# An attention and mixture-of-experts kernel on one core: all sixteen head pairs kept in the rotated column order of memory

## The chip, the cores and the metric
The kernel runs on one core of one Trainium2 chip. The metric is device time in microseconds (us) from launch to end. TensorE is called PE below (PEld is its weight load), VectorE is DVE, ScalarE is ACT, GpSimd is POOL; SyncE (SP) only issues DMAs. SBUF is the on-chip memory of 128 partitions, PSUM the eight accumulator banks that PE writes.

## The reference
Inputs are float32: q, k, v of shape (4, 8, 576, 64), that is 4 batches of 8 heads. Cut to what matters:

```python
q_rot, k_rot = rotate(q), rotate(k)            # rotary embedding: two products and a sum per element
scores = scale * q_rot @ k_rot.T               # per head, 576 x 576
attn = exp(scores - rowmax); attn /= attn.sum(-1) + 1e-9
x = (attn @ v) as (2304 tokens, 512)
logits = x @ phi                               # 32 slots
slots = softmax over tokens(logits).T @ x      # then 8 experts, w1 relu w2, on 4 slots each
x = softmax over slots(logits) @ slot_out
out = relu(x @ w_in) ** 2 @ w_out              # 512 -> 2048 -> 512, 2304 tokens
```

## The kernel before, in words
The 32 heads are worked as sixteen pairs (`p` = 0 to 15, four pairs a batch): the even head of a pair lies on partitions 0 to 63, the odd head on 64 to 127, with the 576 positions along the columns. The work of a pair:

- `load` brings k, q and their swapped halves into one of two buffers `raws[p % 2]`, and `load_v` brings v into `vraws[p % 2]`. All are issued from SP.
- `rope_pair` (six 128x576 operations on POOL) rotates, `parts_pair` splits the result into a rounded part `hi` (ACT) and a rest `lo` (POOL).
- `max_unit` (L535) makes scores from `hi` alone, nine units a pair, and DVE takes their row maxima (L546); `max_rows` (L558 to L584) turns these into a row that a DMA brings back to SBUF (`mrow`).
- `st_unit` (L607, L614) makes the full scores less the maximum, and ACT takes the exponent (L627). Nine units a pair.
- `pv_unit` (L655, and L650 for the last 64 keys of both heads) multiplies by v into two accumulator banks: `obank0` (printed obank_94) for query columns 0 to 287, `obank1` (obank_95) for 288 to 575. These halves are called h = 0 and h = 1. The L650 unit of the next pair opens the accumulation in obank1.
- `norm` for each half: PE sums the exponents (L676), DVE transposes the sums (L682), inverts them (L688 to L691), transposes back (L702), and `scaled` (L698) multiplies the accumulator by the inverse and writes `xT`.
- `logits`: PE multiplies `xT` by phi (L726, L731) and transposes it (L749); after every fourth pair `slots_in` (L780 to L854) folds the batch into the slots.

The maximum, score, sum, logit and transpose units share a ring of three two-bank PSUM buffers (printed bank_91 to bank_93). A unit can start only when the reader of an earlier one has released a buffer.

The host stores the odd head's columns rotated by 64: key positions 512 to 575 come first, so that the two heads' 64-wide tails fall on different partitions. Pairs 0 to 3 (`p < TURNED`, `TURNED = 4`) stay in that order on chip. Their `load` is one DMA over all 128 partitions; their `load_v` is six DMAs that move runs of 256 bytes; `scaled` turns the odd head back as it writes `xT`, in three instructions for h = 0 (64x288, 64x64, 64x224) and two for h = 1 (64x288 each). Their rotary table, in the same order, lies in an extra buffer that a weight slot lends (`claim("w7")`, printed w__134). Pairs 4 to 15 are turned as they are loaded: three DMAs of 64 partitions each (`SEGS`), one contiguous DMA for v, one 128x288 instruction for `scaled`, and a second rotary table brought by `natural_table` (L1109) after the first maxima.

What sets the order: every operation is handed to `Plan.op` with an engine, a cost and a due time. `Plan.retime` shifts the due times by numbers in `UNITS`, `TABLE` and `SHIFT`; `Plan.emit` then issues the operations greedily: of those that could start next, the one due first, where an operation that keeps PE in its present kind of work (`mode`) gains `STAY`. The kinds are r (maxima and scores), c (value products), q (sums, logits, slots) and f (transposes). What results is one fixed instruction list per engine. The same planner places `prepare`, eight conversions of double-precision weights beside the pairs from the fourth on, each with two DVE steps (L1053, L1065), and the weight loads (`free`, L1002).

After the pairs come the experts and the two large products of the last layer (L1659), which use neither the rotary tables nor the pairs' buffers.

Of the kernel before, what the change touches and what calls it, by code (L numbers as in the profile page):

```python
# [9 lines left out]
F32 = mybir.dt.float32  # L10
# [9 lines left out]
B, H, S, D = 4, 8, 576, 64  # L20
# [18 lines left out]
class Plan:  # L39
# [8 lines left out]
    GAP = 0.5  # L48
    LEAVE = 0.09
    ENTER = {"r": 0.11, "c": 0.05, "q": 0.03, "f": 0.05, "b": 0.07, None: 0.05}  # L50
    STAY = 20.522
    AHEAD = 0.208
    UNITS = {
        ("st_unit", "PE", "r"): ("st", 0.0, 0), ("st_unit", "ACT", None): ("st", -9.501, 0), ("pv_unit", "PE", "c"): ("pv", 0.0, 0),
        ("max_unit", "PE", "r"): ("mx", 0.0, 13), ("max_unit", "DVE", None): ("mx", -58.652, 13),
    }
    TABLE = {
# [5 lines left out]
    }  # L63
    SHIFT = {
        ("norm", "PE", "q", False): 5.334,
        ("norm", "DVE", None, False): -51.924,
        ("logits", "PE", "q", False): 1.283,
        ("logits", "PE", "f", False): 3.961,
        ("logits", "DVE", None, False): -5.107,
        ("logits", "ACT", None, False): 1.109,  # L70
        ("max_rows", "PE", "f", False): -1.5,
        ("max_rows", "DVE", None, False): -14.126,
        ("slots_in", "PE", "f", False): 3.47,
        ("slots_in", "PE", "q", False): 2.384,
        ("slots_in", "DVE", None, False): -0.857,
        ("slots_in", "ACT", None, False): -1.093,
        ("rope_pair", "POOL", None, False): 1.035,
        ("parts_pair", "ACT", None, False): 0.251,
        ("parts_pair", "POOL", None, False): -1.618,
        ("load_v", "SP", None, False): 0.738,  # L80
        ("load", "SP", None, False): 0.879,
        ("st_unit", "POOL", None, False): -1.049,
        ("windows", "ACT", None, False): 0.494,
        ("norm", "PE", "q", True): 0.475,
        ("norm", "DVE", None, True): 1.892,
        ("logits", "PE", "q", True): 0.0,
        ("logits", "PE", "f", True): 0.0,
        ("logits", "DVE", None, True): 0.373,
        ("logits", "ACT", None, True): -1.901,
        ("slots_in", "PE", "f", True): -1.785,  # L90
        ("slots_in", "PE", "q", True): 0.0,
        ("slots_in", "DVE", None, True): 2.47,
        ("slots_in", "ACT", None, True): -0.248,
    }
    kind = None

# [167 lines left out]
def kernel(  # L264
# [104 lines left out]
    def dma(fn, due, kb, reads=(), writes=(), after=None, on="SP", behind=None):  # L369
        return op({on: 0.5}, lambda e: fn(), due, reads, writes, kb=kb, after=after, behind=behind)  # L370
# [26 lines left out]

    TURNED = 4  # L400
    early = []
    SEGS = ((slice(0, 64), slice(0, S), slice(0, S)), (slice(64, 128), slice(0, 512), slice(64, S)), (slice(64, 128), slice(512, S), slice(0, 64)))

    def load(p, g, ts_, on="SP", after=None, first="SP"):

        i = p % 2
        if p < TURNED:
            dma(
                lambda: QUEUE[on].dma_start(out=raws[i][:, ts_, :], in_=qk[p][:, ts_, :]),
                g, 1152 * len(range(4)[ts_]) / 4, (), [("raw", i, t, s) for t in range(4)[ts_] for s in range(3)], on=on, after=after,  # L410
            )
            return
        for s, (rows, to, of) in enumerate(SEGS):
            q = on if s else first
            dma(
                lambda rows=rows, to=to, of=of, q=q: QUEUE[q].dma_start(
                    out=raws[i][rows, ts_, to], in_=qk[p][rows, ts_, of]
                ),
                g + 0.01 * s, 1100 * len(range(4)[ts_]) / 4 * (to.stop - to.start) / S, (),
                [("raw", i, t, s) for t in range(4)[ts_]], on=q, after=after,  # L420
            )

    def tt(e, o, x, y, how):
        ENG[e].tensor_tensor(out=o, in0=x, in1=y, op=how)  # L424
# [3 lines left out]
    def rope_pair(p, g):  # L428

        i = p % 2  # L430
        on = {"POOL": 1.39} if p else {"DVE": 0.72}
        if p < TURNED:
            table, tk = (lambda t: early[0][0]()[:, t, :]), [[early[0][1]]] * 2
        else:
            table, tk = (lambda t: rope_sb[:, t, :]), [[("rope", t, s) for s in range(3)] for t in range(2)]
        first = {1: [("hi", 0, 1)], 2: [("mrow", 0, 0), ("mrow", 0, 1)]}.get(p, [])
        for t in range(2):
            a, b = raws[i][:, t, :], raws[i][:, t + 2, :]
            ka, kb = ([("raw", i, n, s) for s in range(3)] for n in (t, t + 2))
# [643 lines left out]
    def at(g, fn, *a):  # L1083
        todo.setdefault(g, []).append((fn, a))
# [4 lines left out]
        return group * first - shift + 0.05 * more  # L1089

    def first_loads():
        ((tab_of, tab_k),) = claim("w7", ([128, 2, S], F32))
        early.append((tab_of, tab_k))
        load(0, -99, slice(0, 4, 2))
        dma(lambda: nc.scalar.dma_start(out=tab_of(), in_=rope.rearrange("t r c -> r t c")), -98.9, 576, (), [tab_k], on="ACT")
        load(0, -98, slice(1, 4, 2))
        load(1, -97, slice(0, 4))
        dma(lambda: nc.sync.dma_start(out=ident, in_=ident_in), -96.5, 65, (), ["ident"])
# [4 lines left out]

        op({"DVE": 0.3}, apart, -20, ["ident"], ["apart"])

    def natural_table():
        for n, (rows, to, of) in enumerate(SEGS):
            dma(
                lambda rows=rows, to=to, of=of: nc.sync.dma_start(out=rope_sb[rows, :, to], in_=rope[:, rows, of].rearrange("t r c -> r t c")),  # L1109
                -2 + 0.01 * n, 550 * (to.stop - to.start) / S, (), [("rope", t, n) for t in range(2)], behind=rows_done[0],  # L1110
            )

    at(-100, first_loads)
    at(-4.1, natural_table)
    at(-4.2, lambda: op({"SP": 1.3}, lambda e: load_consts(), -7, (), ["phi"], kb=200, behind=rows_done[0]))
    for p in range(NP):
        g0 = NU * p
# [707 lines left out]
```

## Time and profile before

| what | value |
|---|---|
| three runs | 572.42, 572.80, 574.49 us; median 572.8 |
| the profiled execution | 571.77 us, span 570.0 us between first and last instruction |
| TensorE clock, mean | 0.991 of full speed |
| first full-score matmul (L607) | 20.17 us |
| last transposes of the pairs (L749) | 290.08 us |
| experts' first products (L1375) | 296.52 us |
| last layer's second product (L1659) | from 342.79 us to the end |

The pairs take some 270 us of the 570. The profile lists instructions per engine with start and duration; `[idle ...]` behind a row is the time for which the engine had stood still and what released it. A busy time of PE includes the tails of pipelined matmuls, so small pauses between units show in start times rather than as idle time.

### The profile page before, as it was taken

What the parts mean: (1) busy time and instruction counts of PE and PEld (TensorE: products, weight loads), DVE (VectorE), ACT (ScalarE), POOL (GpSimd) and SP (SyncE); (2) the same over time, 40 slices, a digit from 0 to 9 for tenths busy, and PEclk for the clock granted to TensorE, in tenths of its full rate; (3) what the DMA queues carried; (4) which work ended last, traced back from release to release, by engine and by line L of the source; (5) the groups of instructions that cost most, each with busy time, mean ns of one, the idle gap of its engine ahead of it and who ended that gap; (6) DMA issues with size and microseconds to landing.
All of it is one profiled execution on the core that took longest, in us unless ns stands there. A gap on an engine that the chain in (4) does not pass through costs nothing.

```text
span 570.0 us, 13340 instructions
## 1 busy us (share of the span) xinstructions
PE 551.7 (97%) x5486; PEld 421.8 (74%) x5486; DVE 384.7 (67%) x836; ACT 283.1 (50%) x528; POOL 220.2 (39%) x173
## 2 busy tenths in 40 slices
PE   3999999999999999999999999999999999999996
PEld 2656666576666667666643358999999999999996
DVE  6587788888888878776475129954784495454553
ACT  2334455654555664534423138964944564444440
POOL 4999999987888888621200000000000000000000
PEclk9699999999999999999999999999999999999999
DMA  6547796867785356245679997222200120000333
GB/s 235 152 125 189 169 238 181 228 174 212 194 228 118 102 135 180 96 174 176 218 258 386 387 396 272 75 75 75 75 1 1 75 75 1 0 2 1 112 112 112
DMA packets 41838, 85.69 MB, mean 150 GB/s; under 512 B 12176, under 2 KB 12848, under 8 KB 40624
## 3 DMA queue, kind: packets, MB, share of 16 engines
q1 hardware_dynamic: 41494, 84.24, 47.6%
q8 instruction: 43, 0.70, 0.5%
q10 hardware_dynamic: 282, 0.59, 0.3%
q14 instruction: 19, 0.16, 0.1%
HBM read 77.92 MB, written 6.82 MB: 149 GB/s over the span
## 4 chain that ended last, share of the span: by engine, by line
PE 89%; DVE 6%; DMA 1%; issue 1%; ACT 1%; SPq 0%; DVEq 0%; ACTq 0%
PE bank L1659 35%; PE obank L655 11%; PE bank L607 11%; PE bank L676 6%; PE bank L535 5%; PE bank L614 3%; DVE mcol L546 3%; PE obank L1589 3%; PE bank L1375 3%; PE bank L1437 2%; PE obank L650 2%; PE bank L749 2%; DMA ident<-in_ident_dram 1%; PE bank L726 1%; PE obank L1521 1%
## 5 line engine op out<-in xcount | busy, mean ns | idle before, releaser
L627 ACT ACTIVATE tO<-bank 128x576 f32<-128x576 f32 x144 | 86.3, 650 | 87.1 <-PE bank L614 82.9
L546 DVE TENSOR_REDUCE mcol<-bank 128x2 f32<-128x576 f32 x144 | 103.1, 747 | 20.5 <-ACT tO L627 9.5
L424 POOL TENSOR_TENSOR arena<-arena 128x576 f32<-128x576 f32 x78 | 110.9, 1443 | 7.9 <-DMA arena<-in_qk_dram 7.1
L1659 PE MATMUL bank<-w,tEb 128*128 128x256 f32 x864 | 106.4, 279 | 0.0
L1659 PEld LDWEIGHTS bank<-w,tEb 128*128 128x128 f32 x864 | 103.3, 188 | 2.4 <-issue 1.6
L655 PE MATMUL obank<-tO,pb 128*64 128x288 f32 x512 | 76.3, 419 | 0.0
L635 POOL TENSOR_TENSOR pb<-tO 128x576 f32<-128x576 f32 x32 | 45.9, 1434 | 36.4 <-ACT tO L627 34.7
L1659 PE MATMUL bank<-w,tEa 128*128 128x256 f32 x432 | 53.0, 279 | 0.0
L1659 PEld LDWEIGHTS bank<-w,tEa 128*128 128x128 f32 x432 | 51.6, 188 | 1.0 <-issue 0.8
L1659 PE MATMUL bank<-w,tO 128*128 128x256 f32 x432 | 51.5, 277 | 0.0
L1659 PEld LDWEIGHTS bank<-w,tO 128*128 128x128 f32 x432 | 51.0, 188 | 0.0
L655 PEld LDWEIGHTS obank<-tO,pb 128*64 128x64 f32 x512 | 31.2, 136 | 23.8 <-issue 9.2
L1600 ACT ACTIVATE pb<-obank 128x384 f32<-128x384 f32 x47 | 21.8, 496 | 44.0 <-PE obank L1589 44.0
L1600 ACT ACTIVATE w__1093<-obank 128x384 f32<-128x384 f32 x48 | 21.7, 494 | 36.4 <-PE obank L1589 36.3
L676 PE MATMUL bank<-tO,ones 128*32 128x288 f32 x256 | 36.7, 409 | 0.0
L535 PEld LDWEIGHTS bank<-tEb 64*128 64x128 f32 x180 | 16.3, 184 | 21.9 <-ACT tO L627 4.5
L535 PE MATMUL bank<-tEb 64*128 64x288 f32 x180 | 30.8, 356 | 1.1 <-ACT tO L627 0.5
L424 POOL TENSOR_TENSOR tLb<-arena,tEb 128x576 fp32r<-128x576 f32 x20 | 28.5, 1438 | 1.4 <-ACT tEb L458 1.4
L607 PE MATMUL bank<-tEb 64*128 64x288 f32 x180 | 28.2, 310 | 0.3 <-DVE mcol L546 0.2
L1589 PE MATMUL obank<-x,tO 128*128 128x384 f32 x95 | 27.0, 339 | 0.3 <-DVE tO L1533 0.3
L682 DVE STREAM_TRANSPOSE bank<-bank 128x288 f32<-128x288 f32 x32 | 15.9, 497 | 15.9 <-PE bank L676 15.8
L607 PE MATMUL bank<-tLb,tEb 64*128 64x288 f32 x180 | 26.6, 292 | 0.0
(301 smaller groups left out, 1064.2 us busy)
## 6 DMA issues: line engine op xcount, KB each, us to landing
arena<-in_qk_dram SPq DMA_DIRECT2D x14, 576.0 KB
arena<-in_qk_dram SPq DMA_DIRECT2D x12, 512.0 KB
arena<-in_w_dram SPq DMA_DIRECT2D x8, 512.0 KB
pb<-in_v_dram SPq DMA_DIRECT2D x12, 320.0 KB
arena<-in_qk_dram SPq DMA_DIRECT2D x3, 1152.0 KB
tLb<-in_w_in_dram SPq DMA_DIRECT2D x3, 1024.0 KB
pb<-in_w_in_dram SPq DMA_DIRECT2D x3, 1024.0 KB
w__450<-in_w_dram SPq DMA_DIRECT2D x4, 512.0 KB
```

The costliest lines, as they stand in the source:

```text
L424: ENG[e].tensor_tensor(out=o, in0=x, in1=y, op=how)
L535: nc.tensor.matmul(on_ring(tok)[:, j, 0:HQ], lhsT=x[rows], rhs=hi[rows, 0, HALF[c]], start=(u < BOTH or c == 0), stop=(u < BOTH or c == 1),)
L546: lambda e: nc.vector.tensor_reduce(out=mcol[:, h, :, u], in_=on_ring(tok)[:, :, 0:HQ], op=ALU.max, axis=AX.X),
L607: nc.tensor.matmul(st[:, j, 0:HQ], lhsT=w[rows], rhs=q[y][rows, HALF[c]], start=(i == 0 and (u < BOTH or c == 0)), stop=False,)
L614: nc.tensor.matmul(st[:, j, 0:HQ], lhsT=pick[rows, w : w + 128], rhs=mrow[rows, HALF[c]], start=False, stop=(u < BOTH or c == 1),)
L627: lambda e: nc.scalar.activation(out=pr, in_=on_ring(tok)[:, :, 0:HQ], func=AF.Exp, scale=0.125),
L635: lambda e: nc.gpsimd.tensor_tensor(out=acc, in0=one, in1=pr, op=ALU.add),
L655: nc.tensor.matmul(BANKS[6 + h][o, 0:HQ], lhsT=vr[:, u, j, :], rhs=pr[:, j, :], start=(h == 0 and u == 0), stop=(h == 1 and u == 3))
L676: nc.tensor.matmul(sm[QUAD[2 * j + w], 0:HQ], lhsT=one, rhs=xs_[2 * i + w][:, j, :], start=(i == 0), stop=(i == 1))
L1589: lambda e, i=i, t0=t0: nc.tensor.matmul(BANKS[i][:, 0:384], lhsT=wst_of()[:, 128 * fc : 128 * fc + 128], rhs=cst_of()[:, t0 : t0 + 384], ...
L1600: lambda e, i=i, h=h: nc.scalar.activation(out=rg_of()[:, 0, h], in_=BANKS[i][:, 0:384], func=AF.Relu),
L1659: nc.tensor.matmul(BANKS[c][:, cols], lhsT=gt[:, x, 128 * c : 128 * c + 128], rhs=wo[:, fc % 2, y, cols], start=(fc % FQ == 0 and i == 0 a ...
```

## The change
`TURNED` becomes `NP` (16). So every pair is loaded by one DMA over all partitions, every v by six DMAs, and every `scaled` is three instructions (h = 0) or two (h = 1). The branch with `SEGS` in `load` goes; its two other users (`natural_table`, and the choice of table in `rope_pair`) go too, and the one rotary table is loaded straight into its final place. The planner's numbers are replaced as a whole. The last layer is as before; the printed line numbers of the changed kernel are lower by 13 to 25.

```diff
-    STAY = 20.522
-    AHEAD = 0.208
+    STAY = 38.746
+    AHEAD = 0.207
...
-        "mx": (0.265, 1.712, 4.344, 4.474, 3.597, 2.052, 4.445, 5.88, 1.071),
+        "mx": (8.916, 13.853, 9.584, 11.633, 10.129, 5.789, 11.309, 14.53, 8.455),
...
-        ("load_v", "SP", None, False): 0.738,
+        ("load_v", "SP", None, False): -5.293,
...
-    TURNED = 4
-    early = []
+    TURNED = NP
...
             return
-        for s, (rows, to, of) in enumerate(SEGS):
-            q = on if s else first
-            dma(
-                lambda rows=rows, to=to, of=of, q=q: QUEUE[q].dma_start(
-                    out=raws[i][rows, ts_, to], in_=qk[p][rows, ts_, of]
-                ),
...
-        if p < TURNED:
-            table, tk = (lambda t: early[0][0]()[:, t, :]), [[early[0][1]]] * 2
-        else:
-            table, tk = (lambda t: rope_sb[:, t, :]), [[("rope", t, s) for s in range(3)] for t in range(2)]
+        table, tk = (lambda t: rope_sb[:, t, :]), [[("rope", t, s) for s in range(3)] for t in range(2)]
...
-        ((tab_of, tab_k),) = claim("w7", ([128, 2, S], F32))
-        early.append((tab_of, tab_k))
         load(0, -99, slice(0, 4, 2))
-        dma(lambda: nc.scalar.dma_start(out=tab_of(), in_=rope.rearrange("t r c -> r t c")), -98.9, 576, (), [tab_k], on="ACT")
+        dma(lambda: nc.scalar.dma_start(out=rope_sb, in_=rope.rearrange("t r c -> r t c")), -98.9, 576, (), [("rope", t, s) for t in range(2) for s in range(3)], on="ACT")
...
-    def natural_table():
-        for n, (rows, to, of) in enumerate(SEGS):
...
-    at(-4.1, natural_table)
```

PE, around the first maximum units of pair 2 (`tEb` holds its `hi`; rows of L535 write one maximum unit each, obank rows are value products). Before:

```order
L607 MATMUL bank_93<-tEb 128x288 x2
L607 MATMUL bank_93<-tLb,tEb 128x288 x2
L607 MATMUL bank_93<-tEb,tLb 128x288 x2
L614 MATMUL bank_93<-tEa,pick 128x288 x2
L535 MATMUL bank_92<-tEb 128x288 x2
L535 MATMUL bank_91<-tEb 128x288 x2
L535 MATMUL bank_93<-tEb 128x288 x2
L655 MATMUL obank_94<-tO_83,pb 64x288 x4
L535 MATMUL bank_92<-tEb 128x288 x2
```

The same place now (L520 is the maximum unit, L640 the value product, L661 the sums, L592 and L599 the scores):

```order
L661 MATMUL bank_93<-tO_84,half_ones 32x288
L640 MATMUL obank_95<-tO_83,pb 64x288 x2
L520 MATMUL bank_91<-tEb 128x288 x2
L520 MATMUL bank_92<-tEb 128x288 x2
L520 MATMUL bank_93<-tEb 128x288 x2
L520 MATMUL bank_91<-tEb 128x288 x2
L592 MATMUL bank_92<-tEb 128x288 x2
L592 MATMUL bank_92<-tLb,tEb 128x288 x2
L592 MATMUL bank_92<-tEb,tLb 128x288 x2
L599 MATMUL bank_92<-tEa,pick 128x288 x2
```

Two score units stood ahead of three maxima and a value product behind them; now four maxima stand in a row right behind a half's sums, and the scores follow.

DVE, the second half of pair 7 from the inversion of its sums to its logits (r_89 the inverse, mrow_124 the row of maxima, w__1093 or w__1058 the weight conversion). Before:

```order
L690 TENSOR_TENSOR r_89<-r_89,bank_92 32x9 x4
L691 RECIPROCAL r_89<-r_89 128x9
L546 TENSOR_REDUCE mcol_122<-bank_93 128x2
L702 STREAM_TRANSPOSE pb<-r_89 128x288
L558 TENSOR_REDUCE m_115<-mcol_122 128x10
L698 TENSOR_TENSOR pb<-obank_95,pb 128x288
L546 TENSOR_REDUCE mcol_119<-bank_92 128x2
L571 TENSOR_SCALAR mrow_124<-bank_93 10x128
L576 SCALAR_TENSOR_TENSOR mrow_124<-bank_93,keep_apart,mrow_124 10x64
L738 TENSOR_TENSOR lg_74<-lg_74,bank_92 128x192
```

And now:

```order
L675 TENSOR_TENSOR r_89<-r_89,bank_91 32x9 x4
L676 RECIPROCAL r_89<-r_89 128x9
L531 TENSOR_REDUCE mcol_122<-bank_92 128x2
L687 STREAM_TRANSPOSE pb<-r_89 128x288
L543 TENSOR_REDUCE m_115<-mcol_122 128x10
L683 TENSOR_TENSOR pb<-obank_95,pb 64x288 x2
L531 TENSOR_REDUCE mcol_119<-bank_91 128x2
L556 TENSOR_SCALAR mrow_124<-bank_92 10x128
L561 SCALAR_TENSOR_TENSOR mrow_124<-bank_92,keep_apart,mrow_124 10x64
L1050 SCALAR_TENSOR_TENSOR w__1058<-w__1058 128x512
L723 TENSOR_TENSOR lg_74<-lg_74,bank_91 128x192
```

The scaling became two instructions, and the second step of the weight conversion, which stood ahead of this half's first transpose, now stands between the row of maxima and the logits.

DVE at the end of the last pair (obank_95 is its second half, lg_76 the last batch's logits). Before:

```order
L698 TENSOR_TENSOR pb<-obank_94,pb 128x288
L702 STREAM_TRANSPOSE pb<-r_89 128x288
L698 TENSOR_TENSOR pb<-obank_95,pb 128x288
L738 TENSOR_TENSOR lg_76<-lg_76,bank_91 128x192
L780 TENSOR_REDUCE m_126<-lg_76 128x1
```

And now:

```order
L683 TENSOR_TENSOR pb<-obank_94,pb 64x288
L683 TENSOR_TENSOR pb<-obank_94,pb 64x64
L683 TENSOR_TENSOR pb<-obank_94,pb 64x224
L687 STREAM_TRANSPOSE pb<-r_89 128x288
L683 TENSOR_TENSOR pb<-obank_95,pb 64x288 x2
L723 TENSOR_TENSOR lg_76<-lg_76,bank_92 128x192
L765 TENSOR_REDUCE m_126<-lg_76 128x1
```

Nothing else changed place here: five scaling instructions stand where two stood.

## Rows read from the trace of the kernel before

**Rows 1.** The page's busy times: us, share of the span, instructions.

```profile
PE 551.7 (97%) x5486; PEld 421.8 (74%) x5486; DVE 384.7 (67%) x836; ACT 283.1 (50%) x528; POOL 220.2 (39%) x173
```

**Rows 2.** Chain of waits in order of time: start, us, what.

```profile
20.24 1.02 PE bank L607 x6
...
77.56 1.11 PE bank L676 x16
...
94.34 1.11 PE bank L676 x16
...
129.66 1.11 PE bank L676 x16
...
145.89 1.11 PE bank L676 x16
...
162.03 1.11 PE bank L676 x16
...
179.98 1.11 PE bank L676 x16
...
290.15 0.71 PE bank L749 x5
```

**Rows 3.** Busy times by stretch: stretch, us, per engine; clock, DMA share, GB/s.

```profile
51.20:68.60 17.40, 17.27 (x203) 10.64 (x196) 13.53 (x35) 7.63 (x16) 17.40 (x14) 1.00 0.64 150
...
145.89:162.03 16.14, 16.14 (x198) 10.73 (x202) 13.42 (x34) 10.30 (x19) 14.02 (x11) 1.00 0.75 208
```

**Rows 4.** Timeline, pair 2's maxima: start, us, engine, line, what, count.

```profile
40.25 0.94 PE L535 MATMUL bank<-tEb 64*128 64x288 f32 x6 [0.24 <-ACT tO L627]
...
41.15 6.08 DVE L546 TENSOR_REDUCE mcol<-bank 128x2 f32<-128x576 f32 x9
...
43.96 0.40 PE L535 MATMUL bank<-tEb 64*128 64x288 f32 x2 [0.27 <-DVE mcol L546]
...
45.29 0.82 PE L535 MATMUL bank<-tEb 64*128 64x288 f32 x4 [0.20 <-DVE mcol L546]
```

**Rows 5.** Groups by line and shape: the scaling; busy, mean ns.

```profile
L698 DVE TENSOR_TENSOR pb<-obank,pb 128x288 f32<-128x288 f32 x24 | 10.9, 454 | 6.0 <-PE obank L655 5.8
L698 DVE TENSOR_TENSOR pb<-obank,pb 64x288 f32<-64x288 f32 x12 | 5.4, 451 | 0.2
L698 DVE TENSOR_TENSOR pb<-obank,pb 64x224 f32<-64x224 f32 x4 | 1.5, 387 | 0.0
L698 DVE TENSOR_TENSOR pb<-obank,pb 64x64 f32<-64x64 f32 x4 | 0.9, 228 | 0.1
```

**Rows 6.** Timeline, pair 7's second half.

```profile
163.36 0.48 DVE L682 STREAM_TRANSPOSE bank<-bank 128x288 f32<-128x288 f32 x1
...
167.39 0.46 DVE L698 TENSOR_TENSOR pb<-obank,pb 128x288 f32<-128x288 f32 x1
...
168.42 0.71 PE L650 MATMUL obank<-tO,pb 64*64 64x288 f32 x8
...
169.18 0.75 PE L749 MATMUL bank<-ident,pb 128*128 128x128 f32 x5
```

**Rows 7.** Timeline, pair 2's second half.

```profile
82.79 0.92 DVE L698 TENSOR_TENSOR pb<-obank,pb 64x288 f32<-64x288 f32 x2
...
83.92 0.72 PE L650 MATMUL obank<-tO,pb 64*64 64x288 f32 x8
```

**Rows 8.** Timeline, the last pair's end.

```profile
289.11 0.46 DVE L698 TENSOR_TENSOR pb<-obank,pb 128x288 f32<-128x288 f32 x1 [1.10 <-PE obank L655]
...
289.62 0.30 PE L726 MATMUL bank<-pb,phi_sb 128*32 128x128 f32 x2 [0.22 <-DVE pb L698]
```

**Rows 9.** DMA issues of v on SP: count, ns min/median/max, first and last start.

```profile
L477 SPq DMA_DIRECT2D pb<-in_v_dram x24: 465/603/1737, 3.4 to 61.6; - x24
L482 SPq DMA_DIRECT2D pb<-in_v_dram x12: 327/328/342, 76.0 to 261.0; - x12
```

**Rows 10.** Waits of the SP queue: us in total, times, longest.

```profile
SPq L584 <- DVE mrow L576: 63.1, 16, 8.2
```

More of the change, by code (lines that the diff above doesn't have):

```diff
@@ L50 @@
     ENTER = {"r": 0.11, "c": 0.05, "q": 0.03, "f": 0.05, "b": 0.07, None: 0.05}
-    STAY = 20.522
-    AHEAD = 0.208
+    STAY = 38.746
+    AHEAD = 0.207
     UNITS = {
-        ("st_unit", "PE", "r"): ("st", 0.0, 0), ("st_unit", "ACT", None): ("st", -9.501, 0), ("pv_unit", "PE", "c"): ("pv", 0.0, 0),
-        ("max_unit", "PE", "r"): ("mx", 0.0, 13), ("max_unit", "DVE", None): ("mx", -58.652, 13),
+        ("st_unit", "PE", "r"): ("st", 0.0, 0), ("st_unit", "ACT", None): ("st", -53.91, 0), ("pv_unit", "PE", "c"): ("pv", 0.0, 0),
+        ("max_unit", "PE", "r"): ("mx", 0.0, 13), ("max_unit", "DVE", None): ("mx", -87.016, 13),
@@ L56 @@
     }
     TABLE = {
[5 rows of a table removed]
[5 rows of a table added]
     }
     SHIFT = {
[L65 to L79, printed above, removed]
-        ("load_v", "SP", None, False): 0.738,
[L81 to L85, printed above, removed]
+        ("norm", "PE", "q", False): 12.303,
@@ new lines @@
+        ("norm", "DVE", None, False): -42.242,
+        ("logits", "PE", "f", False): 9.173,
+        ("logits", "DVE", None, False): 1.345,
+        ("max_rows", "PE", "f", False): -1.538,
+        ("max_rows", "DVE", None, False): -14.332,
+        ("slots_in", "PE", "f", False): 10.484,
+        ("slots_in", "PE", "q", False): 0.192,
+        ("slots_in", "DVE", None, False): -0.45,
+        ("slots_in", "ACT", None, False): -0.389,
+        ("rope_pair", "POOL", None, False): 3.281,
+        ("parts_pair", "ACT", None, False): 1.349,
@@ L86 @@
+        ("parts_pair", "POOL", None, False): 5.432,
+        ("load_v", "SP", None, False): -5.293,
+        ("load", "SP", None, False): 0.952,
+        ("st_unit", "POOL", None, False): 2.631,
+        ("windows", "ACT", None, False): -2.946,
+        ("norm", "PE", "q", True): -2.865,
+        ("norm", "DVE", None, True): 1.214,
         ("logits", "PE", "q", True): 0.0,
         ("logits", "PE", "f", True): 0.0,
-        ("logits", "DVE", None, True): 0.373,
-        ("logits", "ACT", None, True): -1.901,
@@ L90 @@
[L90 to L93, printed above, removed]
+        ("logits", "DVE", None, True): 0.405,
+        ("logits", "ACT", None, True): 0.0,
+        ("slots_in", "PE", "f", True): 0.2,
+        ("slots_in", "PE", "q", True): -0.935,
+        ("slots_in", "DVE", None, True): 0.66,
+        ("slots_in", "ACT", None, True): 0.0,
     }
@@ L412, in load @@
             return
-        for s, (rows, to, of) in enumerate(SEGS):
-            q = on if s else first
-            dma(
-                lambda rows=rows, to=to, of=of, q=q: QUEUE[q].dma_start(
-                    out=raws[i][rows, ts_, to], in_=qk[p][rows, ts_, of]
-                ),
-                g + 0.01 * s, 1100 * len(range(4)[ts_]) / 4 * (to.stop - to.start) / S, (),
-                [("raw", i, t, s) for t in range(4)[ts_]], on=q, after=after,
-            )
     def tt(e, o, x, y, how):
@@ L1104, in first_loads @@
         op({"DVE": 0.3}, apart, -20, ["ident"], ["apart"])
-    def natural_table():
-        for n, (rows, to, of) in enumerate(SEGS):
[L1108 to L1111, printed above, removed]
     at(-100, first_loads)
-    at(-4.1, natural_table)
     at(-4.2, lambda: op({"SP": 1.3}, lambda e: load_consts(), -7, (), ["phi"], kb=200, behind=rows_done[0]))
```

8 rows, old and new, of the table TABLE are left out of this document.

## The prediction

> **What bounds the kernel now.** I read the page's busy times first: PE works for 97% of the span, no other engine for more than 74% of it [rows 1]. So the question is what PE's list costs and where PE pauses. The chain of waits in order of time answers both, since the same unit of a pair returns once a pair. Between the sums at 129.66, 145.89 and 162.03 lie 16.23 and 16.14 us [rows 2]. In the second of these stretches PE is busy for 16.14 of 16.14 us and DVE for 13.42 [rows 3]; I take 16.14 as the price of one pair with nothing lost. The step from 162.03 to 179.98 is 17.95, so folding a batch into the slots adds 1.81. From the first scores (20.24) to the last transposes (290.15) are 269.9 us; sixteen pairs and three such folds make 16 x 16.14 + 3 x 1.81 = 263.7. The rest, 6.2 us, is the ramp at both ends and the pauses, and it is all that the change could win among the pairs, unless it shortened PE's list.
>
> It doesn't. I counted PE's units in both instruction lists: the same number of each, and 207 changes of kind (r, c, q, f) where 208 stood. From the fourth pair on the two lists hold the same units per pair, with neighbours swapped here and there. So the forecast is a sum of pauses.
>
> Where the pauses are: 77.56 to 94.34 is 16.78, 0.64 too long; 94.34 to 129.66 is 35.32, which is two pairs, one fold and 1.23; 129.66 to 145.89 is 0.09 too long. That makes 1.96 us in pairs 3 to 6. Before that, at pair 2's maxima, PE stands idle for 0.24 + 0.27 + 0.20 = 0.71 us, waiting for buffers of the ring, while DVE works through nine maxima without a gap (6.08 us, 0.68 each) [rows 4].
>
> **The change part by part.** *Loads.* For twelve pairs three qk DMAs become one and one v DMA becomes six. An issue of v took 603 ns in the six-part form and 328 ns as one [rows 9], so SP gains at most 6 x 0.60 - 0.33 = 3.3 us a pair, less two qk issues. SP's list also carries the row of maxima that the next pair's scores need; there SP stood waiting for 63.1 us in 16 times, 3.9 each [rows 10], so the 3.3 fit in front of it. I take 0. If a v piece should stand blocked ahead of that row, the scores would wait; the bound from the other side is those 3.3 us twelve times, which I find far off, because the 3.9 would have to be gone.
>
> On the DMA engines the pairs with contiguous v moved 208 GB/s at a busy share of 0.75, those with v in pieces 150 GB/s at 0.64 [rows 3]: 277 against 234 GB/s per full share. Were all traffic of a pair as slow as the second, 208 x 16.14 = 3360 KB would take 14.3 us of 16.14, still less than the pair. The Trainium skill speaks against this part: DMA: Bandwidth & Descriptors (Specifications) wants runs of at least 512 bytes for line rate, and the new v runs are 256. By its rule alone DMA time grows; the row agrees in direction, and as the share stays under 1 the sum is the same by either.
>
> *The rotary table.* Three DMAs behind the first maxima go, with their place on SP. No row shows anyone waiting for what stood behind them, so 0 (POOL has other work queued then); at best it removes some ramp, inside the 6.2.
>
> *Scaling.* Twelve pairs pay on DVE for h = 0 one 64x288, one 64x64 and one 64x224 (451 + 228 + 387 ns) instead of one 128x288 (454 ns), so 0.61 more, and for h = 1 two of 451, 0.45 more [rows 5]: 1.06 a pair, on top of DVE's 13.42 of 16.14 [rows 3], 14.5 in all. DVE keeps 1.6 us to spare. But three PE steps wait for the scaling. (a) The next pair's first unit into obank0 stands well behind the h = 0 scaling in the list. (b) The L650 unit opens obank1 and needs the h = 1 scaling: in pair 7 that began at 167.39, took 0.46, and L650 followed at 168.42, 0.57 later [rows 6]. (c) The transposes at 169.18 have 0.76 more. So 0.45 of the 0.57 at (b) is used up. Does a matmul follow within the 0.12 that are left? Pair 2, already in the split form, answers: scaling from 82.79 for 0.92, to 83.71, and L650 at 83.92, 0.21 later, with no idle time in the row [rows 7]. In addition the conversion's second step moves from ahead of this half's first transpose to behind the row of maxima, so the chain starts no later than at 163.36. I take 0 for these pairs. From both sides: 0, and the whole 0.45 in each of the eleven pairs 4 to 14, 5.0 us.
>
> At the end nothing hides it. In the last pair DVE waits 1.10 us for PE before its h = 1 scaling, and the last logits wait for that scaling [rows 8]; the extra 0.45 goes onto the path whole (the h = 0 scaling's 0.61 falls into the 1.10). Cost 0.45, between 0 and 0.6, because part of the logits used to start before the second half was scaled.
>
> *The conversion's second step* now stands ahead of the logits' accumulation on DVE. That accumulation releases a ring buffer, which the next pair's first maximum takes. The gap between the row of maxima and the logits is what covers it; DVE's slack of 1.6 a pair says it fits, so 0. If not, a part of the eight such places is lost (below).
>
> *Due times.* At pair 2 four maxima now stand right behind a half's sums. The sums hold one of three buffers until DVE has transposed and inverted them. In pair 7 DVE goes from that transpose (163.36) to the scaling (167.39) [rows 6] in 4.0 us, of which three maxima in between take 3 x 0.68: up to 2.0 us are a half's own steps. The third maximum in a row thus waits for that buffer, and the fourth for DVE. That may cost more than the 0.71 shown today or, as the scores behind them then run through, less: between -0.7 and +0.9, and I take -0.3, near the row's own size. In pairs 3 to 6 the regular order now begins one pair earlier, but DVE is fuller there; I take half of the 1.96 as won, -1.0, with 0 and -1.96 as ends.
>
> Sum: -1.0 - 0.3 + 0.45 = -0.85 us. After the pairs nothing changes: the experts' loads are released by the pairs' last units and move with them. Against the profiled execution's own 571.77 (span 570.0 and 1.8 around it) this gives 570.9. Its time is 1.0 below the median of the runs, 572.8; the median is what will be compared, so I predict 572.8 - 0.8 = 572.0. What a measurement of this kernel can tell from no change is about 0.5%, 2.9 us.
>
> **The rivals.** *A, the pauses go.* Some of the 6.2 us are pauses that the busy times hide, and a wholesale new set of due times could remove most of them: -1.96 - 0.7 and another 1.5 of the ramp, +0.45 at the end, -3.7, so 569.1. For it: the regular order begins earlier. Against it: DVE, which PE waited for at pair 2, gets more work, not less.
>
> *B, slower: L650 waits for the split scaling.* Place: the h = 1 scaling in pairs 4 to 14. It decides from the point where the scaling ends less than about 0.2 us (the 0.21 of pair 2) before L650 would start. Price: up to 0.45 x 11 + 0.45 at the end, 5.4, less 1.3 of pauses won: +4.1, 576.9. Half of it: 574.4. For it: only 0.12 us are left by the rows of pair 7, and these pairs carry two conversion steps that pair 2 did not. Against it: pair 2 itself, and the moved second step.
>
> *C, the accumulation of logits comes late.* The step (about 1 us by the stretch it fills) delays the ring buffer in eight pairs; if 0.4 of it shows each time, +3.2 - 0.85: 575.1.
>
> *D, the change doesn't do what it says:* v lands late. A pair then waits on its first value product, and the DMA rule of the skill is its reason. Were the v issues' 3.3 us exposed in only one pair in three: 4 x 3.3 - 0.85 = +12, 585. Against it: the share of 0.75 above.
>
> **How the numbers follow.** Forecast 0.60, own range 570.6 to 574.3 (all ends of the pauses' terms and of the end's term taken together: -1.96 - 0.7 + 0.45 and 0 + 0.9 + 0.6); A 0.14; B 0.13; C 0.09; D 0.04. A reaches past 569.9 with most of its chance, and a little of the forecast does: faster 0.16. B past 575.7 with two thirds, C with a third, D whole: slower 0.15. Same 0.69. The range from 568.6 to 576.0 takes in A nearly whole, half of B and most of C.
>
> **What would show it.** The sums of two neighbouring pairs 16.1 to 16.3 us apart after the sixth pair, without idle time at L650's successor (now L635): B wrong. A step of 16.5 or more there, with PE's weight load released by DVE's scaling (L683): B right. The gap before the first maximum behind the logits: C. POOL or PE idle with in_v as releaser: D. The last logits 0.45 later behind the last value products than before: the end's term. PE's idle time at pair 2's four maxima: the due times' term. A difference of more than 1 us behind the last transposes would make my split of the kernel wrong.

## The result: slower by 0.7%, and most of it lost where nothing was changed

The changed kernel takes 576.86 us (median of 12 runs), the kernel before 573.16 in the same comparison: ratio 1.007, interval 1.0047 to 1.0093. I had forecast 572.0 and a range up to 576.0, with 0.15 for slower. Four of the runs reported below took clearly longer than the others of their kernel (582 to 1058 us, one of them at a mean granted clock of 0.56); medians leave them out, and layout_scale, whose profiled execution was one of them, has no stage times.

The profiled executions are 570.0 us (before) and 575.4 us (after) from the first to the last instruction, 5.4 apart. Lines of the changed kernel's pairs stand 15 lower than before, those behind the pairs 25 lower. The page's busy times, to be held against [rows 1]:

```profile
PE 554.5 (96%) x5490; PEld 423.2 (74%) x5490; DVE 399.9 (69%) x874; ACT 283.6 (49%) x526; POOL 221.8 (39%) x173
```

DVE has 15.2 us more, in 38 more instructions: 36 from the split scaling, and two that ACT had before. The chain of waits in order of time (start, us, what), to be held against [rows 2]:

```profile
20.27 1.02 PE bank L592 x6
...
94.49 1.11 PE bank L661 x16
...
112.65 1.11 PE bank L661 x16
...
145.78 1.11 PE bank L661 x16
...
162.07 1.11 PE bank L661 x16
...
180.48 1.11 PE bank L661 x16
...
197.04 1.11 PE bank L661 x16
...
213.35 1.11 PE bank L661 x16
...
229.85 1.11 PE bank L661 x16
...
292.16 0.71 PE bank L734 x5
```

Up to 162.07 the two kernels are level (162.03 before). Then pairs take 16.56, 16.31 and 16.50 us where 16.14 was the price, and the last transposes come at 292.16, 2.0 late. The other 3.4 us are lost behind them. The start of PE's first expert product (L1375 before, L1350 after) goes from 296.52 to 298.53, the start of its very last product (L1659, L1634) from 565.14 to 570.54: 268.6 us between the two before, 272.0 after. I call this length the back part. No line of it was edited.

Where the back part loses: busy times by stretch (us, per engine; clock, DMA share, GB/s), the first ten us of the last layer before, and the same ten us, 2 us later, after.

```profile
340.00:345.00 5.00, 4.89 (x44) 3.60 (x44) 4.94 (x9) 4.58 (x9) 0.00 (x0) 1.00 1.04 408
345.00:350.00 5.00, 5.00 (x44) 4.26 (x41) 4.94 (x7) 3.88 (x8) 0.00 (x0) 1.00 0.89 311
```

```profile
342.00:347.00 5.00, 4.47 (x37) 3.69 (x37) 4.89 (x10) 4.14 (x8) 0.00 (x0) 1.00 1.04 409
347.00:352.00 5.00, 4.61 (x37) 3.79 (x36) 4.94 (x8) 3.31 (x6) 0.00 (x0) 1.00 1.00 340
```

PE runs 74 products instead of 88 in those ten us. DVE is just as busy in both, so it does the same amount of something less urgent. The timeline of DVE says what. Before:

```profile
339.56 0.29 DVE L1533 TENSOR_TENSOR tO<-obank,tO 64x128 fp32r<-64x128 f32 x1 [0.84 <-ACT tO L1538]
339.88 1.22 DVE L1564 TENSOR_TENSOR w<-arena,w 128x1024 fp32r<-128x1024 f32 x1
341.03 1.02 DVE L1611 TENSOR_TENSOR pb<-pb 128x384 f32<-128x384 f32 x2
341.96 1.02 DVE L1634 TENSOR_TENSOR tEb<-pb,tEb 128x384 fp32r<-128x384 f32 x2
342.90 0.77 DVE L1244 TENSOR_SCALAR arena<-tLb 128x1024 uint16<-128x1024 uint16 x1
```

After (L1508 is L1533 before, L1539 L1564, L1586 L1611, L1609 L1634, L1219 and L1227 are L1244 and L1252):

```profile
339.51 2.35 DVE L1539 TENSOR_TENSOR w<-arena,w 128x1024 fp32r<-128x1024 f32 x2
341.90 0.29 DVE L1508 TENSOR_TENSOR tO<-obank,tO 64x128 fp32r<-64x128 f32 x1
342.22 0.78 DVE L1219 TENSOR_SCALAR arena<-tLb 128x1024 uint16<-128x1024 uint16 x1
342.88 0.74 DVE L1227 TENSOR_SCALAR arena<-tLb 128x1024 uint16<-128x1024 uint16 x1
343.64 1.03 DVE L1586 TENSOR_TENSOR pb<-pb 128x384 f32<-128x384 f32 x2
```

Two steps of a weight conversion (tLb, a piece of w_in that has just landed) now stand ahead of the squares of the first relus, and a split of w_out ahead of the correction of w' that PE's first product reads. ACT shows the same, after:

```profile
342.06 1.17 ACT L1214 ACTIVATE tAX<-tLb 128x1024 f32<-128x1024 f32 x1 [0.59 <-DMA tLb<-in_w_in_dram]
343.14 0.47 ACT L1575 ACTIVATE pb<-obank 128x384 f32<-128x384 f32 x1
```

Before, the relu came first:

```profile
340.38 0.49 ACT L1600 ACTIVATE pb<-obank 128x384 f32<-128x384 f32 x1 [0.86 <-PE obank L1589]
...
342.13 1.15 ACT L1239 ACTIVATE tAX<-tLb 128x1024 f32<-128x1024 f32 x1
```

After the change ACT stands idle 0.59 us for the landing of w_in, converts, and only then computes the relu (343.14) of a product that PE began at 342.25; before, the relu at 340.38 followed a product begun at 339.91. The Trainium skill, Perfetto Trace Analysis (Sequencer Loop), says that a sequencer reads the next instruction and pushes it into its engine's queue, where it waits for its semaphores; the 0.59 us agree. The back part does the same operations in both kernels, but two copies behind the relus went from ACT to DVE, and about 200 of ACT's 236 and of DVE's 231 places in the list hold another operation.

### The profile page after: what moved, and what is told of

Its sections match the earlier page's. It is cut to its first block, busy times and chain, and to the rows that moved or that the text cites. A ratio compares the mean times of both kernels' runs of the same rounds, so it can differ in the third digit from the quotient of the medians.

```text
span 575.4 us, 13430 instructions
## 1 busy us (share of the span) xinstructions
PE 554.5 (96%) x5490; PEld 423.2 (74%) x5490; DVE 399.9 (69%) x874; ACT 283.6 (49%) x526; POOL 221.8 (39%) x173
## 3 DMA queue, kind: packets, MB, share of 16 engines
q1 hardware_dynamic: 50086, 83.65, 42.4%
## 4 chain that ended last, share of the span: by engine, by line
PE 88%; DVE 7%; DMA 3%; issue 1%; ACT 1%; SPq 0%; DVEq 0%; ACTq 0%
PE bank L1634 32%; PE bank L592 12%; PE obank L640 12%; PE bank L661 6%; PE bank L520 5%; PE bank L599 4%; PE bank L1350 3%; PE obank L1564 3%; PE bank L1412 2%; DVE mcol L531 2%; PE obank L635 2%; PE bank L734 2%; DMA ident<-in_ident_dram 1%; DMA w__4726<-in_w_out_dram 1%; PE bank L711 1%
## 5 line engine op out<-in xcount | busy, mean ns | idle before, releaser
L412 POOL TENSOR_TENSOR arena<-arena 128x576 f32<-128x576 f32 x90 | 129.4, 1461 | 15.5 <-DMA arena<-in_qk_dram 15.1
L1634 PE MATMUL bank<-w,tEb 128*128 128x256 f32 x864 | 106.5, 279 | 0.8 <-ACT w__1816 L1651 0.8
L1634 PEld LDWEIGHTS bank<-w,tEb 128*128 128x128 f32 x864 | 103.5, 188 | 3.4 <-issue 1.6
L640 PE MATMUL obank<-tO,pb 128*64 128x288 f32 x512 | 76.4, 419 | 0.0
L1634 PE MATMUL bank<-w,tEa 128*128 128x256 f32 x432 | 53.7, 280 | 0.3 <-DVE tEa L1609 0.3
L1634 PEld LDWEIGHTS bank<-w,tEa 128*128 128x128 f32 x432 | 52.0, 188 | 1.5 <-issue 0.8
L1634 PE MATMUL bank<-w,tO 128*128 128x256 f32 x432 | 51.6, 277 | 0.0
L1634 PEld LDWEIGHTS bank<-w,tO 128*128 128x128 f32 x432 | 51.1, 188 | 0.0
L640 PEld LDWEIGHTS obank<-tO,pb 128*64 128x64 f32 x512 | 31.0, 136 | 23.8 <-issue 9.1
L661 PE MATMUL bank<-tO,ones 128*32 128x288 f32 x256 | 36.7, 409 | 0.0
L683 DVE TENSOR_TENSOR pb<-obank,pb 64x288 f32<-64x288 f32 (+2 forms) x80 | 30.3, 394 | 5.3 <-PE obank L640 4.4
L520 PE MATMUL bank<-tEb 64*128 64x288 f32 x180 | 30.0, 346 | 1.3 <-DVE mcol L531 0.9
L520 PEld LDWEIGHTS bank<-tEb 64*128 64x128 f32 x180 | 16.6, 184 | 19.2 <-issue 6.9
L592 PE MATMUL bank<-tEb 64*128 64x288 f32 x180 | 29.6, 325 | 0.5 <-DVE mcol L531 0.5
L1564 PE MATMUL obank<-x,tO 128*128 128x384 f32 x95 | 26.9, 338 | 0.9 <-DVE tO L1508 0.9
L592 PE MATMUL bank<-tEb,tLb 64*128 64x288 f32 x180 | 26.5, 291 | 0.0
```

Source lines behind the costliest of these rows:

```text
L520: nc.tensor.matmul(on_ring(tok)[:, j, 0:HQ], lhsT=x[rows], rhs=hi[rows, 0, HALF[c]], start=(u < BOTH or c == 0), stop=(u < BOTH or c == 1),)
L592: nc.tensor.matmul(st[:, j, 0:HQ], lhsT=w[rows], rhs=q[y][rows, HALF[c]], start=(i == 0 and (u < BOTH or c == 0)), stop=False,)
L640: nc.tensor.matmul(BANKS[6 + h][o, 0:HQ], lhsT=vr[:, u, j, :], rhs=pr[:, j, :], start=(h == 0 and u == 0), stop=(h == 1 and u == 3))
L661: nc.tensor.matmul(sm[QUAD[2 * j + w], 0:HQ], lhsT=one, rhs=xs_[2 * i + w][:, j, :], start=(i == 0), stop=(i == 1))
L683: nc.vector.tensor_tensor(out=xT[rows, to : to + b - a], in0=BANKS[6 + h][rows, a:b], in1=recT[rows, a:b], op=ALU.mult)
L1564: lambda e, i=i, t0=t0: nc.tensor.matmul(BANKS[i][:, 0:384], lhsT=wst_of()[:, 128 * fc : 128 * fc + 128], rhs=cst_of()[:, t0 : t0 + 384], ...
```

## The experiments

All were run beside the kernel before. The table gives, from the profiled execution, the start of the last transposes, the last pair (from the transposes before them to these), and the back part; then the median and the ratio to the kernel before with its interval (the kernel before was run beside each group of runs, hence the range of its medians).

| kernel | last transposes | last pair | back part | median us | ratio |
|---|---|---|---|---|---|
| before | 290.1 | 5.64 | 268.6 | 573.2 to 572.3 | 1 |
| after | 292.1 | 6.11 | 272.0 | 576.9 | 1.0070 (1.0047 to 1.0093) |
| tail_old | 292.6 | 6.11 | 268.8 | 574.4 | 1.0024 (0.9994 to 1.0053) |
| tail_new | 291.0 | 5.64 | 271.6 | 574.8 | 1.0026 (0.9999 to 1.0054) |
| layout | 303.2 | 6.11 | 274.1 | 589.1 | 1.0275 (1.0233 to 1.0316) |
| tables | 299.6 | 5.64 | 268.6 | 582.6 | 1.0169 (1.0121 to 1.0218) |
| layout_scale | - | - | - | 587.1 | 1.0246 (1.0231 to 1.0261) |
| layout_v | 305.7 | 6.11 | 273.3 | 589.3 | 1.0290 (1.0259 to 1.0321) |
| tail_old_scale | 292.4 | 5.64 | 268.7 | 574.1 | 1.0030 (1.0016 to 1.0044) |
| tail_old_v | 291.6 | 6.11 | 268.6 | 574.0 | 1.0026 (1.0005 to 1.0047) |
| tail_old_both | 291.9 | 5.64 | 269.7 | 573.8 | 1.0017 (0.9995 to 1.0039) |
| frozen | 293.1 | 6.11 | 268.6 | 575.4 | 1.0045 (1.0027 to 1.0062) |
| frozen_one | 297.9 | 5.64 | 268.6 | 575.3 | 1.0032 (0.9995 to 1.0068) |
| mend | 290.7 | 6.11 | 268.8 | 574.0 | 1.0016 (0.9996 to 1.0036) |
| cost04 | 302.1 | 6.11 | 268.8 | 584.7 | 1.0220 (1.0175 to 1.0266) |

**The order behind the pairs: tail_old, tail_new.** The planner is told which of the back part's instructions is next on PE, ACT and DVE; tail_old is the changed kernel with the old list, tail_new the old kernel with the new list.

```
...
+                    if i >= self.tail and e in self.FORCED and (nxt[e] >= len(self.FORCED[e]) or self.FORCED[e][nxt[e]] != i - self.tail):
+                        continue
...
```

> The changed kernel, with the 926 instructions behind the attention pairs on PE, ACT and DVE forced into the order they had in the kernel before. In the two traces the changed kernel's last transposes come 2.0 us late, its last product 5.4 us late, so 3.4 us go behind the pairs. Theory T1 (the new order of the last layer's conversions, squares and relus makes in-order ACT and DVE wait for weights with PE's work queued behind): 576.9 - 3.4 = 573.5 us, and PE's last product 2.0 us behind that of before. Rival T2 (the weights land later because the loads' stretch starts 2 us later; the order is beside the point): 576.9 us, no change. Rival T2b (the forced order only shifts the wait to another operation): between the two, about 575.

> The kernel before, with PE, ACT and DVE forced into the changed kernel's order behind the pairs; the pairs are untouched. T1: 573.2 + 3.4 = 576.6 us, all of the growth behind the experts' last product. T2: 573.2 us, since the pairs end when they did and the loads with them. In between (574 to 575.5): order and lateness of the weights both take part.

Measured: the back part goes from 272.0 to 268.8 us in tail_old and from 268.6 to 271.6 in tail_new. So 3.0 to 3.2 us follow the list, in whichever kernel it stands. The medians move by less than I had put down for tail_new (+2.3, not +3.4) and leave 2.0 over in tail_old.

**The two halves of the change: layout, tables.** layout is the changed kernel with the due times of before; tables is the kernel before with the due times of after.

```
-    STAY = 38.746
+    STAY = 20.522
...
-        "st": (9.466, 8.073, 9.996, 6.129, 11.1, 10.228, 9.417, 10.271, 7.867),
+        "st": (1.952, 0.685, 2.425, -0.609, 3.608, 3.906, 1.691, 0.712, 2.095),
```

> The changed kernel with the due times of the kernel before: rotated layout, whole loads and split scaling alone. Its order behind the pairs is, instruction for instruction, the changed kernel's. T1: 3.4 us of loss behind the pairs, plus at least the 0.5 us of the last scaling: 577.1 us or more; if the pairs' other 1.5 us come from the layout too (theory P1: the split scaling and the later landing loads cost the pairs), 578.6; if they come from the due times (P2), 577.1. T2: as T1 less the 3.4 where the pairs end no later than before, about 574.

> The kernel before with the changed kernel's due times: no rotated loads past pair 3, no split scaling past pair 3. Its order behind the pairs is, instruction for instruction, that of the kernel before. T1: nothing lost behind the pairs. P1 (layout costs the pairs 1.5 us): the pairs end where they did, 573.2 us or up to 1 less. P2 (due times cost them): 574.7 us, last transposes 1.5 us late. T2: 573.2 plus as much again behind the pairs as the pairs end late.

Measured: each half alone is far worse than the whole, +13.2 and +9.6 us at the last transposes. I had expected 0 to 2. The due times belong to the layout. And T2 falls: in tables the pairs end 9.6 us late, the loads released by them with it, and the back part is 268.6 us to the tenth, in the old order. In layout, which has the new order behind the pairs, it is 274.1; 2.4 of that lie ahead of the experts' last product, where the mean granted clock from 300 to 352 us is 0.90, between the levels of 1.2 and 2.4 GHz, behind stretches at 1.00; layout_v's 273.3 likewise holds a stretch at 0.93 (352 to 400 us).

**What costs inside the pairs: layout_scale, layout_v, tail_old_scale, tail_old_v, tail_old_both.** The scaling of pairs 4 to 15 as one instruction, or their v in one transfer, in the planner's unchanged order.

```
-            if p < TURNED:
+            if p < 4:
                 parts = [(HEADS[0], 0, HQ, HQ * h)] + ...
```

```
-                    lambda j=j, ...: nc.sync.dma_start(out=vraws[i][to, ut, j, :], in_=v[p][of, uf, j, :]),
+                    lambda n=n, j=j, ...: nc.sync.dma_start(out=vraws[i][to, ut, j, :], in_=v[p][of, uf, j, :]) if p < 4 else nc.sync.dma_start(out=vraws[i], in_=v[p]) if n == 0 else None,
```

> The run layout (589.1 us) with the scaling of pairs 4 to 15 as one 128x288 instruction in the same place of the order; the odd head's columns of those pairs then stay rotated, so that part of the output is left wrong. Layout alone lost 13 us up to the last transposes (303.7 against 290.6 and 291.5). Theory S (DVE, 36 of 40 us busy there, is filled by the split scaling and PE waits for its maxima and accumulations): nearly all of the 13 goes, 577 us. Theory V (v in six pieces holds up SP and so the loads behind them, POOL waits): 588 us. Theory R (neither; the order that the planner writes for the new costs is itself worse): 588 us too.

> The run layout (589.1 us) with v of pairs 4 to 15 loaded by one transfer of 2560-byte runs in the place of the first of the six pieces; the odd head's v of those pairs then stays unrotated, so that part of the output is left wrong. Theory V: POOL's wait for the loads falls from 20.6 us to about 7, as before the change, and 577 us. Theories S and R: 588 to 589 us, though POOL's wait may fall.

> The run tail_old (574.4 us) with the scaling of pairs 4 to 15 as one instruction, as in layout_scale (same part of the output left wrong). Last pair: 6.10 us from the second last transposes to the last falls back to 5.64 (both theories). Theory S: pairs 7 to 14 also fall back to 16.15 us each from 16.25 to 16.55, and 573.0 us. Theory L (due times set longer runs of logits, whose products wait for the three banks in turn): only the last pair's 0.5 goes, 573.9 us.

> The run tail_old (574.4 us) with v of pairs 4 to 15 in one transfer, as in layout_v (same part of the output left wrong). Theory V: POOL's wait for the loads falls from 15 us to about 7 and the 1.2 us of pairs 8 to 11 go, 573.2 us. Theories S and L: POOL's wait falls, PE does not wait for POOL, 574.4 us.

> The run tail_old (574.4 us) with v of pairs 4 to 15 in one transfer and their scaling as one instruction, both as before (parts of the output left wrong). Theory L (the pairs' remaining 1.2 us come from the order that the new due times set): last pair back to 5.64 us, steady pairs still 16.25 us, 573.9 us. If the two together are what costs (each alone covered by the other): steady pairs 16.15 us and 572.8 us.

Measured: neither brings layout's 13 us back (-2.1 and +0.2), so S and V both fall there and R is left; frozen, below, tests R itself. POOL's wait for the loads hardly shrinks with v whole (19.7 us in layout_v, 20.6 in layout). On tail_old the last pair falls back to 5.64 us with the one scaling, as both theories had it. The steady pairs do not fall back: from the transposes of pair 10 to those of pair 11 it takes 16.24 us in tail_old, 16.26 with the scaling whole, 16.25 with v whole and 16.25 with both, against 16.15 before. The step ahead of it is shorter with both undone (16.25 against 16.48 to 16.56). From pair 7's transposes to pair 12's are 86.4 us in tail_old, 85.6, 85.3 and 85.4 with the scaling, v and both undone, and 84.3 before; after and mend (below), whose instruction lists of the pairs are those of tail_old, take 85.8 and 85.3. So 1.0 us stays whatever is undone, which is theory L; what lies above it is within the spread of one list. Its 573.9 was measured as 574.1 and 573.8. The back part of tail_old_both has 1.0 too much: there the piece of w_in landed 9.3 us after its issue and PE waited 1.4 us for the correction of w'. So late weights can cost something in the old order too, once in nine profiles that have it.

**The layout in the old order: frozen, frozen_one.** frozen emits the changed loads, v pieces (six, one behind the other) and scalings from the old plan, so that no other instruction changes place.

```
-            lambda: nc.sync.dma_start(out=vraws[i], in_=v[p]), g, 327,
+            six, g, 327,
...
-            if p < TURNED:
+            if True:
                 parts = [(HEADS[0], 0, HQ, HQ * h)] + ...
```

> The kernel before in its own order on every engine, instruction for instruction, with only the layout changed in it: all pairs loaded whole, the rotary table loaded once more in rotated form, v of pairs 4 to 15 in six pieces issued back to back where the one transfer stood, their scaling split. The run layout (589.1 us) had these changes and the planner's new order for them. Theory O (the layout itself costs little, the order that the planner writes with it costs the 13 us): 573 to 574 us, 0.5 of it in the last pair. Theory C (the layout's costs add up on DVE and SP, whatever the order): 580 us or more.

> The run frozen with the scaling of pairs 4 to 15 as one 128x288 instruction; their odd heads' columns then stay rotated, and that part of the output is left wrong. Theory O: 0.5 us less than frozen, all in the last pair, about the kernel before. Theory C with the split scaling as the main cost: as the kernel before, frozen 5 us or more above it. If v's six pieces are what costs: as frozen.

Measured: 575.4, 3.1 us above the kernel before, where layout is 16.7 above it. Theory O holds in the main: four fifths of what the layout costs under the old due times is the order that the planner writes with it, within the pairs and behind them. C in its strong form (580) falls, but O's 573 to 574 was too low: DVE's longer list does cost PE 0.2 to 0.4 us in several pairs of frozen (16.53, 16.47, 16.32 where 16.15 stood), plus two waits of 1.0 and 0.9 us for DVE's maxima. With one scaling (frozen_one) three steady pairs are back at 16.15 us and the last at 5.64, but two others take 16.80 and 16.85; its profile has one pause of PE of 4.6 us in pair 3, and its runs spread from 571.6 to 579.8, so its median says nothing about frozen's 3.1. In that pause ACT waits 6.8 us for a step of a staged weight conversion on DVE. layout waits for the same step:

```profile
ACT w__1059 L1047 <- DVE w__1059 L1040: 17.2, 8, 5.8
```

(us in total, times, longest). What makes it come and go is open.

**The smallest edits: mend, cost04.** mend adds one dependency that only the planner sees. cost04 sets one number of the planner back and emits what the changed kernel emits.

```
-                f64(cs[n % 2][k], raw_of, due, rk, start if n else None)
+                f64(cs[n % 2][k], raw_of, due, rk, relus[0] if n == 1 else start if n else None)
...
```

```
-            {"DVE": 0.8 if p < TURNED else 0.4},
+            {"DVE": 0.8 if p < 4 else 0.4},
```

> The changed kernel with one dependency more for the planner: the conversion of w_in's second quarter is not placed before the first relu of the last layer. Its order behind the pairs then differs from that of the kernel before in one neighbouring pair of instructions on ACT and one on DVE. T1 in its narrow form (T1n: that conversion, in front of the first relus, is what costs): as tail_old, 574.4 us, 268.7 us from the experts' first product to the last. If other parts of the new order cost too (T1w): 575 to 576.5.

> The changed kernel with one number of the planner set back: the scaling of pairs 4 to 15 is planned at 0.4 instead of 0.8 on DVE; what is emitted is the changed kernel's split scaling. Behind the pairs the planner then writes the order of the kernel before, instruction for instruction; within the pairs some neighbours change places too. If the planned cost is what flipped the order (theory F): 268.6 to 268.9 us from the experts' first product to the last, against 272.0, and 573.5 to 574.5 us in all. If the chip's own lateness takes part: over 270 us there. The pairs may gain or lose up to 1 us by their own neighbours' new places; no theory says which.

Measured: mend has a back part of 268.8 us and 574.0 in all; to pin the conversion of w_in's second quarter behind the first relu gives back all of the 3.2 us (T1n); the other 200 places follow from it. In mend's first ten us of the last layer PE has 85 products (74 in after, 88 before):

```profile
341.00:346.00 5.00, 4.89 (x44) 3.66 (x45) 4.05 (x8) 4.53 (x9) 0.00 (x0) 1.00 1.03 409
346.00:351.00 5.00, 5.00 (x41) 4.32 (x42) 4.94 (x8) 3.85 (x7) 0.00 (x0) 1.00 0.77 248
```

cost04 has the old order behind the pairs and 268.8 us there, which settles theory F: the planner's 0.4 us more for each split scaling is what flipped the list of the last layer. Yet the kernel takes 584.7. The same number had kept the pairs in order: planned at 0.4, the list gives the interval that ends with pair 4's transposes half as many products of kind q again as before (96 for 64). That interval takes 22.2 us (18.2 in after), the next 14.5 (16.8), the two behind them 19.9 and 17.3 (16.3 each). I had allowed 1 us for that.

No version beat the kernel before; mend comes closest.

## Why the prediction was wrong, step by step

**"After the pairs nothing changes: the experts' loads are released by the pairs' last units and move with them."** This is the step that failed: I put the back part at 0, and it holds 3.4 us of the growth, of which 3.0 to 3.2 follow the order of its list alone (mend, tail_old, tail_new). The loads did move with the pairs. But the back part is written by the same greedy planner in the same pass, and a different cost ahead of it gave ACT and DVE another order. I had compared the two lists up to the last pair only. The last sentence of my section on what would show it named this case (more than 1 us behind the last transposes); the profile met it.

**Due times: -1.0 in pairs 3 to 6 and -0.3 at pair 2's maxima.** The second is mis-sized, in sign too; the first stays open. From pair 2's transposes to pair 7's are 84.42 us before (84.76 to 169.18) and 84.49 after (84.73 to 169.22): 0 won of 1.96 between these two profiles. But the same two lists of pairs were profiled again: the old one takes 85.54 in tail_new, the new one 84.17 in tail_old and 83.96 in mend, so a gain of the size that I forecast is not excluded. At pair 2, PE after (start, us, idle time and releaser in brackets):

```profile
37.53 0.53 PE L520 MATMUL bank<-tEb 64*128 64x288 f32 x4 [0.29 <-ACT tEb L443]
38.22 0.40 PE L520 MATMUL bank<-tEb 64*128 64x288 f32 x2 [0.16 <-DVE r L675]
39.48 0.40 PE L520 MATMUL bank<-tEb 64*128 64x288 f32 x2 [0.87 <-DVE mcol L531]
40.15 0.40 PE L592 MATMUL bank<-tEb 64*128 64x288 f32 x2 [0.27 <-DVE mcol L531]
```

These are 1.59 us instead of 0.71 [rows 4], close to the +0.9 that I gave as the bad end. The mechanism was the one described, a third maximum waiting for DVE's steps on the sums' buffer (0.16) and a fourth for DVE (0.87); the value that I chose had the wrong sign. The first transposes are none the later for it (55.20 against 55.92), nor are pair 2's.

**Steady pairs cost 16.14 whatever the due times.** Not so: 16.25 to 16.56 from pair 8 on. Undoing the scaling and v, apart and together, leaves 1.0 us over pairs 8 to 12, so that much lies in the new order within the pairs. Which of its neighbours' places costs is open; in pairs 11 to 13 the gaps between PE's starts of consecutive score products add up to 9.60 us (9.02 before, 158 gaps in both), without an idle time in a row, and the other gaps shrink by 0.32. One list doesn't end at one time, though: the last transposes of the old list came at 290.1 and 291.0 (tail_new, mostly by one wait of 1.0 us in pair 3), those of the new list at 292.1, 292.6 (tail_old) and 290.7 (mend).

**Scaling: 0 in steady pairs, 0.45 at the end.** Right in the order that the planner wrote. In the old order (frozen) the same split does cost several pairs 0.2 to 0.4. Pair 7 after:

```profile
167.43 0.92 DVE L683 TENSOR_TENSOR pb<-obank,pb 64x288 f32<-64x288 f32 x2
...
168.46 0.72 PE L635 MATMUL obank<-tO,pb 64*64 64x288 f32 x8
...
169.22 0.75 PE L734 MATMUL bank<-ident,pb 128*128 128x128 f32 x5
```

The scaling ends at 168.35 and L635 begins 0.11 later with no idle time: the 0.12 that [rows 6] left were enough, and pair 2's form [rows 7] was the right row to judge by. So B is wrong, though its 576.9 is by chance the measured time; a total that agrees proves no mechanism. The end, after:

```profile
290.65 0.92 DVE L683 TENSOR_TENSOR pb<-obank,pb 64x288 f32<-64x288 f32 x2 [0.37 <-PE obank L640]
...
291.63 0.31 PE L711 MATMUL bank<-pb,phi_sb 128*32 128x128 f32 x3 [0.69 <-DVE pb L683]
```

PE waits 0.69 where it waited 0.22 [rows 8], and the last pair is 0.47 longer. In tail_old_scale it is 5.64 us again and the wait 0.22:

```profile
291.43 0.46 DVE L694 TENSOR_TENSOR pb<-obank,pb 128x288 f32<-128x288 f32 x1 [1.04 <-PE obank L651]
...
291.95 0.30 PE L722 MATMUL bank<-pb,phi_sb 128*32 128x128 f32 x2 [0.22 <-DVE pb L694]
```

**Loads: 0.** Right for PE. POOL's wait for qk grew from 7.1 to 15.1 us and hid behind its own slack; v whole gains nothing that can be measured, and D is wrong. My bound on the DMA engines was not. From the two stretches of [rows 3] I took 277 GB/s per full share for v in one transfer and 234 for v in pieces. The same two stretches after, both with v in pieces:

```profile
51.20:68.60 17.40, 17.40 (x201) 11.01 (x199) 14.24 (x37) 8.52 (x18) 16.91 (x13) 1.00 0.54 171
145.77:162.02 16.25, 16.25 (x199) 10.75 (x198) 14.63 (x37) 9.76 (x18) 14.89 (x11) 1.00 0.66 208
```

171 at 0.54 and 208 at 0.66 are 317 and 315 per full share, more than either before, so v in pieces cannot be what held the first stretch at 234. The Trainium skill, DMA: Bandwidth & Descriptors (Specifications), asks for at least 512 bytes for line rate. By that rule the new v runs cost DMA time, and the pages show it: the queue of the loads (packets, MB, share of the 16 engines' time) in before, frozen, tail_old and tail_old_v, in this order:

```profile
q1 hardware_dynamic: 41494, 84.24, 47.6%
q1 hardware_dynamic: 50358, 84.24, 42.4%
q1 hardware_dynamic: 50086, 83.65, 42.2%
q1 hardware_dynamic: 35302, 83.65, 41.1%
```

With v of twelve pairs whole again, the same bytes take 41.1% instead of 42.2, some 7 us of the engines' time in the whole run (42.2% of 572.8 less 41.1% of 571.5), hidden as far as the medians tell (574.4 and 574.0). What outweighs this is the other half of the new loads: frozen, which has v in pieces and packets under 512 bytes doubled (12,176 to 24,880), but k and q of a pair and the rotary table in one DMA each, takes 42.4% where the kernel before takes 47.6 for the same bytes.

**The accumulation of logits (C), the rotary table.** The steps from 145.78 to 180.48 (16.29 and 18.41, with one fold of 1.81) leave 0.6 us in two pairs, and no row of the steady pairs names a buffer that waits for the accumulation. C's 0.4 in eight places isn't there. No wait in either trace names the load of a rotary table.

In sum, between profiles: +3.4 behind the pairs, +0.5 at the last pair, +1.5 in the order within the pairs. The third is the least sure: by the same reckoning mend, with the same list of pairs, has 0.2 there and tail_old 2.0. The medians are 3.7 apart; mend, which gives the first term back, leaves 1.7 (574.0 against 572.4) with a ratio of 1 inside its interval, so of the other two terms the medians tell little, and it is tail_old_scale's profile that shows the second.

## What to carry to other kernels

Where a planner or a scheduler writes the lists, an edit reaches every instruction that is planned after it: compare the lists to the last row, also where no line was changed, and ask of each engine that waits for loads what now stands queued behind the wait. Tables of due times are fitted to one set of costs; layout and due times cost 13 and 10 us apart and 2 together, so judge neither alone, and pin the order (as frozen does) to price an edit by itself. A work of low urgency that "fits in a gap" should get an explicit predecessor, because the gap is in the plan and the landing of its data is not.

## What the runs showed of the chip

One DMA over 128 partitions for k and q of a pair, in place of three over 64, and one instead of three for the second rotary table lowered the DMA engines' share of the run from 47.6% to 42.4% for the same 84.24 MB (before and frozen), although v in six pieces, which by itself costs about 1 point (tail_old against tail_old_v), came with it. One and the same list of pairs ended 0.9 us apart in two profiles (old list) and 1.9 us apart in three (new list), while the back part repeated within 0.3 us in eight of nine profiles with the old order, wherever the pairs had ended between 290 and 302 us.
